# Full-height products for the rest channels, and equal weights side by side

## The chip, the cores and the metric

The kernel runs on one core of a Trainium2 chip. The metric is the device time of one execution in microseconds (us), as the median of several runs. All inputs are drawn at random with a fixed seed.

## What is computed

A tensor x of 2 x 4096 tokens with 192 channels goes through three steps. The first is a causal convolution over 7 tokens, with one softmaxed row of taps for each of 8 groups of 24 channels. The second and third are two gated layers of the same shape, 192 to 2048 to 192, with different gates.

```python
def _moe_ref(x, w_in, w_out):
    h = x @ w_in                          # 8192 x 192 by 192 x 2048
    relu6 = np.clip(h + 3.0, 0.0, 6.0)
    g = h * relu6 / 6.0
    return (g @ w_out).astype(np.float32)

def _moe2_ref(x, w_in, w_out):
    h = x @ w_in
    g = np.where(h > 0.0, h, np.exp(np.minimum(h, 0.0)) - 1.0)
    return (g @ w_out).astype(np.float32)
...
    x = attn_out.reshape(B * S, D)
    x = _moe_ref(x=x, **moe_kwargs)
    return _moe2_ref(x=x, **moe2_kwargs)
```

The result is wanted in float32. The weights of the layers arrive as 64-bit floats and are rounded on the chip.

## The kernel before

**Tiles.** Tokens are worked in 16 blocks of 512 (256 of each batch), hidden channels in 16 chunks of 128. One block in one chunk of one layer is a *slot*; there are 512. A slot's first product gives h (128 hidden channels by 512 tokens, `mm1`, line 359, its matmuls on line 368). `gate` (line 371) makes g of it, with one or two ScalarE steps into a tile u and one VectorE step. `split_g` (line 383) makes the parts gh (ScalarE) and gl (VectorE). `mm2` (line 392) multiplies these by the second weights, on lines 401 to 405 in layer 1 (five matmuls of 512 columns) and on lines 413 and 416 in layer 2 (eight matmuls, of 384 and 192 columns in turn).

**Parts.** Each float32 operand is split exactly into a high and a low part of the type float32r, and a product is the sum of high x high, high x low and low x high in float32 PSUM. Of the 192 input channels, the first 128 are the tiles opA (high) and opB (low), against the weights wi-h (high) and wi-l (low). The remaining 64, the *rest channels*, fill only half of the 128 rows. They stand twice over the partitions: opC (`lh`) has the low parts on rows 0 to 63 and the high parts on rows 64 to 127, opD (`hl`) the other way round. Their weights wi-r stand as high over low for the even chunks and as low over high for the odd ones.

So a chunk has five matmuls: wi-h with opA, wi-l with opA, wi-h with opB, and two for the rest. For an even chunk, wi-r with opC at full height gives both mixed products, and the upper-left half of wi-r (rows 0 to 63) with the same rows of opD gives high x high, at half height. For an odd chunk it is wi-r with opD at full height and rows 64 to 127 of wi-r with those of opC.

```python
if f % 2 == 0:
    todo = [(w["h"], A), (w["l"], A), (w["h"], Bt), (w["r"], lh), (w["r"][LO], hl[LO])]
else:
    todo = [(w["r"][UP], lh[UP]), (w["r"], hl), (w["h"], A), (w["l"], A), (w["h"], Bt)]
```

**Order.** `two` (line 591) works two slots at a time, the even chunk and the odd one: both first products, then the second products of the two slots before. As an even chunk ends with its half-height matmul and an odd one begins with its own, the two stand together, one on the upper and one on the lower half of the rows. h has two buffers (`ps_h`, line 91), so a chunk's first matmul waits until the gate of the chunk two slots earlier has read its h. Side work (decoding weights, the convolution, evacuations, splits of layer 1's output) is put beside the slots by `run_jobs` (line 450), which counts VectorE's and ScalarE's columns. Layer 1 is worked up to six blocks ahead; then blocks of layer 2 and layer 1 take turns. In the first 94 slots (`OWN`, line 26, some 230 us) the framework's scheduler may reorder instructions on each engine; after them the order written in the program stands. In these slots all weights are decoded, on VectorE and ScalarE. The taps of the first two blocks are done on TensorE (line 257, tile psc), those of the others on VectorE (tile acc).

Lines recorded as L50 are all VectorE and ScalarE instructions, which pass through the counting class `Meter`; they are told apart by their tiles.

Of the kernel before, what the change touches and what calls it, by code (L numbers as in the profile page):

```python
# [30 lines left out]
HB = NB // 2  # L31
# [1 line left out]


class Meter:
    """An engine whose instructions are counted, in columns."""

    def __init__(self, engine, fixed):
        self.engine, self.fixed, self.work = engine, fixed, 0
# [14 lines left out]

@with_exitstack
def conv_moe_moe2(ctx: ExitStack, tc: tile.TileContext, x, weight, w_in1, w_out1, w_in2, w_out2, out):
    """Causal per-head taps, then two gated layers, block of tokens by block.

    Products: an operand is split exactly into float32r hi + lo (12 bits each)
    and hi*hi + hi*lo + lo*hi accumulate in float32 PSUM. Channels 0..127 are  # L60
    operands A (hi) and B (lo); channels 128..191 ("r") stand twice over the
    partitions, C (hi) and D (lo), against weights stacked as [hi; lo].

    The layers' weights come as float64 bits (two 32-bit words each) and are
    rounded to float32 on chip.
    """
    nc = tc.nc
    B, S, D = x.shape
    H, K = weight.shape
# [31 lines left out]
    three = const.tile([P, 1], F32, name="three")  # L101
    taps = const.tile([P, 2, K], F32, name="taps")

# [1 line left out]
    def word(raw, i):  # L105
        return raw.rearrange("p (n two) -> p n two", two=2)[:, :, i]

    def decode(raw, n, meanwhile):
        """float64 -> float32. The exponent is moved by a product with 2^-112 on
        the high word (its top 8 exponent bits are a float32 exponent), the three  # L110
        low exponent bits and the mantissa by a shift; the low word gives the
        three last mantissa bits, rounded."""
        xw = tmp.tile([P, NB], F32, name="xw", tag="xw")
        act.mul(xw[:, :n], word(raw, 1).bitcast(F32), 2.0 ** -112)
        c = tmp.tile([P, NB], I32, name="cw", tag="cw")
        vec.tensor_scalar(out=c[:, :n], in0=word(raw, 0).bitcast(U32), scalar1=2.0 ** -29, scalar2=7.0,
                          op0=ALU.mult, op1=ALU.min)
        yield
        yield from meanwhile
        xi = xw.bitcast(I32)  # L120
        vec.scalar_tensor_tensor(out=c[:, :n], in0=xi[:, :n], scalar=3, in1=c[:, :n],
                                 op0=ALU.logical_shift_left, op1=ALU.bitwise_or)
        yield
        vec.scalar_tensor_tensor(out=xi[:, :n], in0=xi[:, :n], scalar=SIGN, in1=c[:, :n],
                                 op0=ALU.bitwise_and, op1=ALU.bitwise_or)
        yield
        return xw
# [18 lines left out]
        return t[:, :n]  # L146

    def split_w(item, f):
        """Chunks a..e-1 of the hidden channels. The r rows of w_in come with the even
        chunks on the lower partitions and the odd ones on the upper; in wi the even  # L150
        chunks stand as [hi; lo], the odd ones as [lo; hi]."""
        kind, l, a, e = item
        if kind == "out":
            v = f[:, :(e - a) * D].rearrange("p (f e) -> p f e", f=e - a)
            w = wo[l][:, a:e]
            act.copy(w[:, :, 0:D], v)
            yield
            for c0, c1, to in (((0, P, 2 * P), (P, D, D)) if l == 0 else ((0, D, D),)):
                vec.tensor_tensor(out=w[:, :, to:to + c1 - c0], in0=v[:, :, c0:c1],
                                  in1=w[:, :, c0:c1].bitcast(F32), op=ALU.subtract)  # L160
            yield
            return
        w = {k: v[:, a * P:e * P] for k, v in wi[l].items()}
        if kind == "in":
            f = f[:, :(e - a) * P]
            act.copy(w["h"], f)
            yield
            vec.tensor_tensor(out=w["l"], in0=f, in1=w["h"].bitcast(F32), op=ALU.subtract)
        else:
            f = f[:, :(e - a) // 2 * P].rearrange("p (f c) -> p f c", c=P)  # L170
            r = w["r"].rearrange("p (f two c) -> p two f c", two=2, c=P)
            for k, h in enumerate((LO, UP)):
                act.copy(r[h, k], f[h])
            yield
            for k, h, o in ((0, LO, UP), (1, UP, LO)):
                vec.tensor_tensor(out=r[o, k], in0=f[h], in1=r[h, k].bitcast(F32), op=ALU.subtract)
        yield

# [1 line left out]
    def load_taps():  # L180
        raw = const.tile([H, K], F32, name="traw")
        nc.scalar.dma_start(raw, weight)
# [22 lines left out]
        vec.tensor_copy(taps, pt)  # L205
        yield

# [1 line left out]
    # The r channels of batch 0 stand on the lower half of the partitions, those of batch 1 on the upper.  # L209
    x_sb = {}  # L210
    xT = {}
    opnd = {}
# [36 lines left out]
        return a.rearrange("p n t -> p (n t)")  # L249

    def taps_tensor(b, part):
        """The taps as diagonal matrices, in full float32."""
        q = xT[b, part]
        ps = ps_o.tile([P, NB], F32, name="psc", tag="po")
        for n in range(SEG[part]):
            for k in range(K):
                nc.tensor.matmul(ps[:, n * HB:(n + 1) * HB], diag[k], q[:, n, k:k + HB],  # L257
                                 start=k == 0, stop=k == K - 1)
            yield
        return ps  # L260
# [30 lines left out]
    CONV = 2 * K + 6  # L291

    def ring():
        """Operands of one block in one layer: A hi and B lo of channels 0..127;
        the r channels as [lo; hi] and [hi; lo] over the partitions."""
        A = op.tile([P, NB], F32R, name="opA", tag="opA")
        Bt = op.tile([P, NB], F32R, name="opB", tag="opB")
        lh = op.tile([P, NB], F32R, name="opC", tag="opC")
        hl = op.tile([P, NB], F32R, name="opD", tag="opD")
        return A, Bt, lh, hl  # L300
# [4 lines left out]
        yield from transposes(b, pool, tag)  # L305

    def ring():
        """Operands of one block in one layer."""
        A = op.tile([P, NB], F32R, name="opA", tag="opA")
        Bt = op.tile([P, NB], F32R, name="opB", tag="opB")  # L310
        C = op.tile([P, NB], F32R, name="opC", tag="opC")
        Dt = op.tile([P, NB], F32R, name="opD", tag="opD")
        return A, Bt, C, Dt

# [1 line left out]
    SIXTH = 1.0 / 6.0  # L316

    ys = {}

    def evac1(b, p0, p1):  # L320
        """Layer 1's sum, over six (its gate was not divided). p1 holds the r
        channels' hi and lo weight parts on its two halves."""
        y0 = yp.tile([P, NB], F32, name="y0", tag="y0")
        act.mul(y0, p0, SIXTH)
        yield
# [29 lines left out]
            nc.sync.dma_start(out[t0:t0 + P, :], o)  # L355
            yield

# [1 line left out]
    def mm1(l, b, f):  # L359
        A, Bt, lh, hl = opnd[l, b]  # L360
        w = {k: v[:, f * P:(f + 1) * P] for k, v in wi[l].items()}
        h = ps_h.tile([P, NB], F32, name="h", tag="h")
        if f % 2 == 0:
            todo = [(w["h"], A), (w["l"], A), (w["h"], Bt), (w["r"], lh), (w["r"][LO], hl[LO])]
        else:
            todo = [(w["r"][UP], lh[UP]), (w["r"], hl), (w["h"], A), (w["l"], A), (w["h"], Bt)]
        for i, (k, m) in enumerate(todo):
            nc.tensor.matmul(h, k, m, start=i == 0, stop=i == len(todo) - 1)  # L368
        return h
# [49 lines left out]
                for step in (lo, hi) if last else (hi, lo):  # L419
                    step(j)  # L420

# [1 line left out]
    slots = [(0, 0, f) for f in range(STAG)]  # L423
    for f in range(STAG, NF + STAG, 2):
        slots += [(0, 0, f), (0, 0, f + 1)] * (f < NF) + [(0, 1, f - STAG), (0, 1, f - STAG + 1)]
# [16 lines left out]
                    yield  # L442

    def job(gen, n, a, e):
        """A generator of n steps, run after slot a and before slot e."""
        jobs.append([e if callable(e) else lambda: e, a, gen, n, 0])

    debt = [0, 0]

    def run_jobs(s, before):  # L450
        """Side work next to slot s: what is due; in the steady part, each job's even share;
        in the first part as much as keeps the engines at the tensor engine's pace."""
        for i, (eng, w) in enumerate(zip((vec, act), before)):
            debt[i] = min(max(debt[i] - PACE, -PACE), -PACE // 2) + eng.work - w

# [26 lines left out]
        return at[l, 0, a] + (LAG if kind == "out" else 0)  # L482

    def when(i):
        """The slot before which item i is to be there; layer 2's come evenly, ahead of their need."""
        if i >= len(items):
            return 0
        if i < N1:
            return due(items[i]) - LEAD
        return min(due(items[i]) - LEAD, W2[0] + (W2[1] - W2[0]) * (i - N1) // (len(items) - N1))  # L490
# [26 lines left out]
    ready = [0]  # L517

    def prepare():
        """The weights in the order of need, each item's split beside the next one's decoding."""  # L520
        last = iter(())
        for i, item in enumerate(items):
            ahead(i)
# [65 lines left out]
            gs[s] = split_g(raw_g.pop(s))  # L589

    def two(s):
        """Two chunks' first products, so that their half-height ones stand together,
        then the second products of the two before."""
        w = vec.work, act.work
        both = range(s, min(s + 2, NS))
        hs = [mm1(*slots[i]) for i in both]
# [59 lines left out]
```

## Time and profile before

| | before |
|---|---|
| runs | 1274.56, 1274.86, 1274.91 us |
| median | 1274.86 us |
| span of the profiled execution | 1273.5 us |
| TensorE busy (PE) | 1262.9 us, 99%, 6044 matmuls |
| weight loads (PEld) | 973.0 us, 76%, 6044 loads |
| VectorE busy (DVE) | 907.5 us, 71% |
| ScalarE busy (ACT) | 922.1 us, 72% |
| granted TensorE clock | 1.00 over the span |

The span runs from the first instruction to the last; the profiled execution gives no other time of its own. PE stands for TensorE's matmuls and PEld for its weight loads, which are instructions of their own; DVE is VectorE and ACT is ScalarE. A matmul's record begins when it starts; its end is modelled, and records of successive matmuls overlap. The distance from one start to the next therefore says what a matmul takes of TensorE's time, and its record's duration does not.

### The profile page before, as it was taken

To read this page: it belongs to the slowest core of one execution; us is meant where nothing else is said; L and a number is where in the kernel's file an instruction comes from. 1 tells how busy PE (TensorE), PEld (TensorE's weight loads), DVE (VectorE), ACT (ScalarE), POOL (GpSimd) and SP (SyncE) were. 2 spreads that over 40 slices of the span, in tenths; PEclk is the share of its full clock that TensorE was granted. 3 is DMA by queue.
4 is the path that set the end of the run, shared out by engine and by line. 5 is a ranking of instruction groups with operands and counts; after the bars stand their busy time and mean duration, and the time that the engine had idled before them with its cause. 6 is when DMAs were issued, how large, how long until landed. Compare 5 with 4: busy or idle time off the path is not lost.

```text
span 1273.5 us, 17036 instructions
## 1 busy us (share of the span) xinstructions
PE 1262.9 (99%) x6044; PEld 973.0 (76%) x6044; DVE 907.5 (71%) x1557; ACT 922.1 (72%) x1651; POOL 9.5 (1%) x44
## 2 busy tenths in 40 slices
PE   8999999999999999999999999999999999999998
PEld 6777777777787777878778787777877778888887
DVE  7999999766667676676766767667676656666665
ACT  5768777686775867758677585776867677787786
POOL 0000000000000000000000000000000000000000
PEclk9999999999999999999999999999999999999999
DMA  5322110000000000000000000000000000000000
GB/s 166 94 77 59 54 38 13 1 1 26 1 2 24 1 25 2 10 16 1 25 1 23 3 1 26 1 26 1 1 13 1 13 1 8 7 13 13 14 13 13
DMA packets 34581, 26.26 MB, mean 21 GB/s; under 512 B 10816, under 2 KB 33344, under 8 KB 34496
## 3 DMA queue, kind: packets, MB, share of 16 engines
q1 hardware_dynamic: 34480, 25.18, 6.9%
q8 instruction: 47, 0.77, 0.2%
q14 instruction: 38, 0.31, 0.1%
q10 hardware_dynamic: 16, 0.00, 0.0%
HBM read 18.87 MB, written 6.29 MB: 20 GB/s over the span
## 4 chain that ended last, share of the span: by engine, by line
PE 98%; DVE 1%; ACT 0%; DMA 0%; issue 0%; SPq 0%; DVEq 0%
PE h L368 50%; PE po L413 15%; PE po L416 7%; PE p L405 5%; PE p L403 5%; PE p L401 5%; PE p L402 5%; PE p L404 5%; PE psx L229 1%; PE psc L257 0%; DMA x_sb<-in_x_dram 0%; DVE acc L50 0%; ACT u L50 0%; DVE cw L50 0%; DVE diag L50 0%
## 5 line engine op out<-in xcount | busy, mean ns | idle before, releaser
L50 DVE SCALAR_TENSOR_TENSOR g<-u,h 128x512 f32<-128x512 f32 x512 | 351.0, 686 | 322.0 <-ACT u L50 319.9
L50 DVE TENSOR_TENSOR gl<-g,gh 128x512 fp32r<-128x512 f32 x512 | 350.6, 686 | 30.7 <-ACT gh L50 22.3
L50 ACT CAST gh<-g 128x512 fp32r<-128x512 f32 x512 | 314.3, 614 | 45.6 <-DVE g L50 44.0
L50 ACT ACTIVATE u<-h,three 128x512 f32<-128x512 f32 x256 | 175.7, 688 | 183.4 <-PE h L368 182.7
L413 PE MATMUL po<-wo,gh 128*128 128x384 f32 x1024 | 302.2, 358 | 0.0
L416 PE MATMUL po<-wo,gl 128*128 128x192 f32 x1024 | 255.7, 252 | 0.2 <-DVE gl L50 0.2
L50 ACT ACTIVATE u<-h 128x512 f32<-128x512 f32 x256 | 151.3, 591 | 78.7 <-PE h L368 76.1
L416 PEld LDWEIGHTS po<-wo,gl 128*128 128x128 f32 x1024 | 194.9, 191 | 5.4 <-DVE gl L50 0.5
L413 PEld LDWEIGHTS po<-wo,gh 128*128 128x128 f32 x1024 | 192.4, 188 | 5.5
L50 ACT ACTIVATE u<-u 128x512 f32<-128x512 f32 x256 | 161.9, 632 | 8.2
L368 PE MATMUL h<-opD,wi1r 64*128 64x512 f32 (+1 forms) x256 | 119.3, 496 | 0.0
L368 PE MATMUL h<-opD,wi0r 128*128 128x512 f32 (+1 forms) x256 | 118.3, 495 | 0.0
L50 DVE SCALAR_TENSOR_TENSOR acc<-xT,taps,acc 128x256 f32<-128x256 f32 (+1 forms) x180 | 107.0, 602 | 0.0
L368 PEld LDWEIGHTS h<-opD,wi0r 128*128 128x128 f32 (+1 forms) x256 | 47.4, 185 | 76.9 <-issue 76.9
L368 PEld LDWEIGHTS h<-opD,wi1r 64*128 64x128 f32 (+1 forms) x256 | 47.3, 185 | 76.9 <-issue 76.9
L368 PE MATMUL h<-opC,wi1r 128*128 128x512 f32 (+1 forms) x256 | 105.3, 441 | 0.0
L368 PE MATMUL h<-opC,wi0r 64*128 64x512 f32 (+1 forms) x256 | 104.9, 443 | 0.0
L368 PE MATMUL h<-opA,wi1h 128*128 128x512 f32 x256 | 104.0, 406 | 0.0
L368 PE MATMUL h<-opA,wi0h 128*128 128x512 f32 x256 | 102.1, 399 | 0.0
L405 PE MATMUL p<-gl,wo 128*128 128x512 f32 x256 | 102.0, 398 | 0.0
L368 PE MATMUL h<-opA,wi1l 128*128 128x512 f32 x256 | 101.7, 397 | 0.0
L368 PE MATMUL h<-opA,wi0l 128*128 128x512 f32 x256 | 101.7, 397 | 0.0
(86 smaller groups left out, 1648.6 us busy)
## 6 DMA issues: line engine op xcount, KB each, us to landing
raw<-in_moe_w_out_dram SPq DMA_DIRECT2D x16, 384.0 KB, 3.2
out_dram<-o SPq DMA_DIRECT2D x64, 96.0 KB, 1.7
x_sb<-in_x_dram SPq DMA_DIRECT2D x32, 128.0 KB, 2.6
raw<-in_moe_w_in_dram SPq DMA_DIRECT2D x7, 512.0 KB, 3.8
xr_sb<-in_x_dram SPq DMA_DIRECT2D x32, 64.0 KB, 2.3
raw<-in_moe_w_in_dram SPq DMA_DIRECT2D x8, 256.0 KB, 3.9
raw<-in_moe_w_in_dram SPq DMA_DIRECT2D x4, 128.0 KB, 3.2
traw<-in_weight_dram ACTq DMA_DIRECT2D x1, 0.2 KB
```

Source lines behind the costliest of these rows:

```text
L50: return fn(*args, **kw)
L229: nc.tensor.transpose(ps[:, j * P:(j + 1) * P], src, ident)
L368: nc.tensor.matmul(h, k, m, start=i == 0, stop=i == len(todo) - 1)
L401: nc.tensor.matmul(p0, w0h, gh, start=first, stop=False)
L402: nc.tensor.matmul(p0, w0l, gh, start=False, stop=False)
L403: nc.tensor.matmul(p1, wr, gh, start=first, stop=False)
L404: nc.tensor.matmul(p0, w0h, gl, start=False, stop=last)
L405: nc.tensor.matmul(p1, wr, gl, start=False, stop=last)
L413: nc.tensor.matmul(a[j][:, 0:2 * D], gh[:, j * P:(j + 1) * P], w, start=first, stop=last)
L416: nc.tensor.matmul(a[j][:, 0:D], gl[:, j * P:(j + 1) * P], w[:, 0:D], start=False, stop=False)
```

## The change

The list of a chunk's matmuls becomes the same for even and odd chunks. The half-height matmul of the rest channels becomes a full-height one: wi-r with opC and wi-r with opD, both over 128 rows. The full-height product with opD also adds low x low, a part that was left out before. The two matmuls with wi-h now follow each other, and so do the two with wi-r. The diff also takes out comments and docstrings, by which the lines between 57 and `mm1` are numbered one higher; lines 368 to 590 keep their numbers.

```diff
     def mm1(l, b, f):
...
         A, Bt, lh, hl = opnd[l, b]
         w = {k: v[:, f * P:(f + 1) * P] for k, v in wi[l].items()}
         h = ps_h.tile([P, NB], F32, name="h", tag="h")
-        if f % 2 == 0:
-            todo = [(w["h"], A), (w["l"], A), (w["h"], Bt), (w["r"], lh), (w["r"][LO], hl[LO])]
-        else:
-            todo = [(w["r"][UP], lh[UP]), (w["r"], hl), (w["h"], A), (w["l"], A), (w["h"], Bt)]
+        todo = [(w["h"], A), (w["h"], Bt), (w["l"], A), (w["r"], lh), (w["r"], hl)]
         for i, (k, m) in enumerate(todo):
             nc.tensor.matmul(h, k, m, start=i == 0, stop=i == len(todo) - 1)
         return h
```

What this does to the order of instructions shows at three places. The first is TensorE in the steady part, the first products of one pair of chunks of layer 1 (h_2542 is the even chunk's h, h_2548 the odd one's). Before:

```order
L368 MATMUL h_2542<-opA_2132,wi0h_88 128x512
L368 MATMUL h_2542<-opA_2132,wi0l_89 128x512
L368 MATMUL h_2542<-opB_2133,wi0h_88 128x512
L368 MATMUL h_2542<-opC_2134,wi0r_90 128x512
L368 MATMUL h_2542<-opD_2135,wi0r_90 128x512
L368 MATMUL h_2548<-opC_2134,wi0r_90 128x512
L368 MATMUL h_2548<-opD_2135,wi0r_90 128x512
L368 MATMUL h_2548<-opA_2132,wi0h_88 128x512
L368 MATMUL h_2548<-opA_2132,wi0l_89 128x512
L368 MATMUL h_2548<-opB_2133,wi0h_88 128x512
```

The last matmul of h_2542 and the first of h_2548 are the half-height ones (the size shown is that of the output). Now:

```order
L368 MATMUL h_2542<-opA_2132,wi0h_88 128x512
L368 MATMUL h_2542<-opB_2133,wi0h_88 128x512
L368 MATMUL h_2542<-opA_2132,wi0l_89 128x512
L368 MATMUL h_2542<-opC_2134,wi0r_90 128x512
L368 MATMUL h_2542<-opD_2135,wi0r_90 128x512
L368 MATMUL h_2548<-opA_2132,wi0h_88 128x512
L368 MATMUL h_2548<-opB_2133,wi0h_88 128x512
L368 MATMUL h_2548<-opA_2132,wi0l_89 128x512
L368 MATMUL h_2548<-opC_2134,wi0r_90 128x512
```

One matmul of the odd chunk, opD with wi0r, follows behind these rows. Both chunks now have the same order, and the odd one's rest products stand at its end.

The second place is TensorE at the first pair of chunks of all, around the convolution's taps on TensorE (psc). Before:

```order
L257 MATMUL psc_310<-xT0_279,diag0_103 128x256 x3
L368 MATMUL h_290<-opA_99,wi0h_88 128x512
L368 MATMUL h_290<-opA_99,wi0l_89 128x512
L368 MATMUL h_296<-opC_101,wi0r_90 128x512
L368 MATMUL h_296<-opD_102,wi0r_90 128x512
L368 MATMUL h_296<-opA_99,wi0h_88 128x512
L368 MATMUL h_296<-opA_99,wi0l_89 128x512
L257 MATMUL psc_310<-xT0_279,diag0_103 128x256
L368 MATMUL h_290<-opB_100,wi0h_88 128x512
L368 MATMUL h_290<-opC_101,wi0r_90 128x512
L368 MATMUL h_290<-opD_102,wi0r_90 128x512
L368 MATMUL h_296<-opB_100,wi0h_88 128x512
```

Now:

```order
L368 MATMUL h_290<-opA_99,wi0h_88 128x512
L368 MATMUL h_296<-opA_99,wi0h_88 128x512
L258 MATMUL psc_310<-xT0_279,diag0_103 128x256
L258 MATMUL psc_310<-xT0_279,diag1_104 128x256 x2
L368 MATMUL h_290<-opB_100,wi0h_88 128x512
L368 MATMUL h_290<-opA_99,wi0l_89 128x512
L368 MATMUL h_290<-opC_101,wi0r_90 128x512
L368 MATMUL h_290<-opD_102,wi0r_90 128x512
L368 MATMUL h_296<-opB_100,wi0h_88 128x512
L368 MATMUL h_296<-opA_99,wi0l_89 128x512
L368 MATMUL h_296<-opC_101,wi0r_90 128x512
L368 MATMUL h_296<-opD_102,wi0r_90 128x512
```

The products with opA and with the rest channels that stood ahead of the first one with opB now stand behind it.

The third place is VectorE just after, at the gates g of this pair. Before:

```order
L50 SCALAR_TENSOR_TENSOR g_302<-u_303,h_290 128x512
L50 TENSOR_SCALAR acc1_318<-xT1_285,taps_98 128x256
L50 SCALAR_TENSOR_TENSOR g_332<-u_333,h_296 128x512
L50 SCALAR_TENSOR_TENSOR acc1_318<-xT1_285,taps_98,acc1_318 128x256
L50 TENSOR_TENSOR gl_338<-g_302,gh_336 128x512
```

Now:

```order
L50 SCALAR_TENSOR_TENSOR g_302<-u_303,h_290 128x512
L50 TENSOR_SCALAR acc1_318<-xT1_285,taps_98 128x256
L50 TENSOR_TENSOR wi0l_89<-xw_259,wi0h_88 128x512
L50 SCALAR_TENSOR_TENSOR acc1_318<-xT1_285,taps_98,acc1_318 128x256
L50 SCALAR_TENSOR_TENSOR g_332<-u_333,h_296 128x512
L50 SCALAR_TENSOR_TENSOR acc1_318<-xT1_285,taps_98,acc1_318 128x256
L50 TENSOR_TENSOR gl_338<-g_302,gh_336 128x512
```

The low part of one piece of weights (wi0l) is taken ahead of the second gate. A few more steps of VectorE and ScalarE change places within the first 40 us; from there on both engines, and GpSimd and the DMA queue throughout, have the same instructions in the same order as before.

## Rows read from the trace of the kernel before

**Rows 1.** The page: the span, then engine, busy us (share), instructions
```profile
span 1273.5 us, 17036 instructions
PE 1262.9 (99%) x6044; PEld 973.0 (76%) x6044; DVE 907.5 (71%) x1557; ACT 922.1 (72%) x1651; POOL 9.5 (1%) x44
```

**Rows 2.** The page: the chain that ended last, shares by engine and by line
```profile
PE 98%; DVE 1%; ACT 0%; DMA 0%; issue 0%; SPq 0%; DVEq 0%
PE h L368 50%; PE po L413 15%; PE po L416 7%; PE p L405 5%; PE p L403 5%; PE p L401 5%; PE p L402 5%; PE p L404 5%; PE psx L229 1%; PE psc L257 0%; DMA x_sb<-in_x_dram 0%; DVE acc L50 0%; ACT u L50 0%; DVE cw L50 0%; DVE diag L50 0%
```

**Rows 3.** Groups by form: line, engine, tiles, rows*columns, form, count, busy us, mean ns
```profile
L368 PE MATMUL h<-opA,wi0l 128*128 128x512 f32 x256 | 101.7, 397 | 0.0
L368 PE MATMUL h<-opD,wi0r 64*128 64x512 f32 x128 | 63.0, 492 | 0.0
```

**Rows 4.** Timeline of TensorE, a pair of layer 1: start us, duration us, instruction
```profile
619.10 0.39 PE L368 MATMUL h<-opA,wi0h 128*128 128x512 f32 x1
619.10 0.19 PEld L368 LDWEIGHTS h<-opA,wi0l 128*128 128x128 f32 x1
...
619.79 0.39 PE L368 MATMUL h<-opC,wi0r 128*128 128x512 f32 x1
620.12 0.18 PEld L368 LDWEIGHTS h<-opD,wi0r 64*128 64x128 f32 x1 [0.36 <-issue]
620.12 0.49 PE L368 MATMUL h<-opD,wi0r 64*128 64x512 f32 x1
...
620.12 0.49 PE L368 MATMUL h<-opC,wi0r 64*128 64x512 f32 x1
...
620.54 0.50 PE L368 MATMUL h<-opD,wi0r 128*128 128x512 f32 x1
...
620.88 0.40 PE L368 MATMUL h<-opA,wi0h 128*128 128x512 f32 x1
...
621.58 0.39 PE L401 MATMUL p<-gh,wo 128*128 128x512 f32 x1
...
623.93 0.39 PE L368 MATMUL h<-opA,wi0h 128*128 128x512 f32 x1
```

**Rows 5.** Timeline of TensorE in the start, around a lone half-height matmul
```profile
32.18 0.40 PE L368 MATMUL h<-opB,wi0h 128*128 128x512 f32 x1
...
32.51 0.49 PE L368 MATMUL h<-opC,wi0r 64*128 64x512 f32 x1
...
32.93 0.50 PE L401 MATMUL p<-gh,wo 128*128 128x512 f32 x1
...
33.27 0.40 PE L402 MATMUL p<-gh,wo 128*128 128x512 f32 x1
...
33.50 0.40 PE L368 MATMUL h<-opD,wi0r 128*128 128x512 f32 x1
...
33.74 0.39 PE L368 MATMUL h<-opC,wi0r 128*128 128x512 f32 x1
```

**Rows 6.** Windows: us, each engine's busy us (instructions), granted clock, DMA share, GB/s
```profile
20.00:220.00 200.00, 200.00 (x838) 145.18 (x837) 187.35 (x348) 149.02 (x270) 2.86 (x8) 1.00 0.22 63
...
180.00:200.00 20.00, 20.00 (x88) 14.61 (x87) 19.72 (x37) 16.43 (x30) 0.44 (x2) 1.00 0.22 62
```

**Rows 7.** VectorE's waits, 20 to 220 us: us in total, times, longest
```profile
DVE g L50 <- ACT u L50: 8.7, 25, 0.9
```

**Rows 8.** Timeline at the start of a layer-2 block: ScalarE, VectorE, TensorE
```profile
576.64 0.60 ACT L50 ACTIVATE u<-h 128x512 f32<-128x512 f32 x1 [0.48 <-PE h L368]
...
580.44 0.69 DVE L50 SCALAR_TENSOR_TENSOR g<-u,h 128x512 f32<-128x512 f32 x1 [1.82 <-ACT u L50]
...
580.89 0.49 PE L368 MATMUL h<-opD,wi1r 64*128 64x512 f32 x1
...
581.18 0.49 PE L368 MATMUL h<-opC,wi1r 64*128 64x512 f32 x1
```

**Rows 9.** Timeline of VectorE: the low part of block 0's first operand
```profile
19.98 0.67 DVE L50 TENSOR_TENSOR opB<-psc,opA 128x512 fp32r<-128x512 f32 x1
```

## The prediction

> **What bounds the kernel now.** I read the page's table of busy times first: TensorE is busy for 1262.9 of 1273.5 us, VectorE and ScalarE for 71% and 72% [rows 1]. The chain that ended last says the same: 98% of it is TensorE, and half of the whole chain is line 368, the first products, which the change rewrites [rows 2]. So what one TensorE slot costs is paid nearly in full at the end, and the question is how long the slots around the half-height matmuls are. A record's own duration does not tell that, because matmuls overlap: the half-height ones have a mean of 492 ns [rows 3], yet a full-height one starts every 0.23 us. I therefore read distances between starts in the timeline.
>
> One pair of chunks stands in [rows 4]. The ten second products run from 621.58 to 623.93, where the next pair begins: 2.35 us, 0.235 each. The ten first products, with as many columns each, run from 619.10 to 621.58: 2.48 us. The difference sits in one place: from opC full height (619.79) over the two halves (both 620.12) and opD full height (620.54) to the next opA (620.88) pass 1.09 us, for four matmuls. The two halves do run together, starting within 0.01 us. But before them stand 0.33 us, after them 0.42, and one matmul further still 0.34. The rows of the weight loads show why: a load normally starts together with the matmul ahead of its own (the load for wi0l at 619.10, the start of the matmul on wi0h; it is used 0.23 us later), while the first half's load starts at 620.12, together with its own matmul, after 0.36 us without a load ("issue": nothing else was waited for). Around a change of height the load is no longer hidden behind a matmul.
>
> **The change, part by part.**
>
> *Two halves become two full-height matmuls.* There are four groups of 128 half-height matmuls, one of which is shown [rows 3]: 512, in 256 pairs. Now: 1.09 us for the four matmuls around each pair. After: four full-height starts at the plain distance, 4 x 0.235 = 0.94. That is 0.15 less per pair, and 256 x 0.15 = **38.4 us less**. The opposite price, two slots where the halves shared one, is in this sum: the 0.94 counts all four. A row of a full-height rest product right behind another one is rare in the trace, but there is one, in the start: opD full at 33.50, opC full at 33.74, 0.24 apart [rows 5]. Starts are shown to 0.01 us, so the 0.15 may be off by 0.01: 2.6 us each way.
>
> By the Trainium skill ("TensorE: Matmul & The Clock Gate", Part 3: Packing small matmuls) matmuls in different row groups run side by side and a pack lasts one matmul plus some 4 ns for each further one. Of this the trace bears out the start, within 0.01 us, but not the length: by that rule alone the halves would cost one slot, giving them up would add an estimated 0.23 us per pair, and the kernel would end some 59 us later.
>
> *The order inside a chunk.* wi-h against opA, then opB, then wi-l, then the rest. No matmul is added, and no load falls away in the program: each matmul call brings its own load, before and after, 6044 of each [rows 1]. Plain starts are 0.23 to 0.24 apart whichever weights follow, so I put this at nothing; the second load of the same weights hides behind the matmul ahead as any other does. What it would be if not is a rival below.
>
> *VectorE and ScalarE.* Their work is the same, so a faster TensorE leaves them less time. It matters between 20 and 220 us, where the weights are decoded: VectorE is busy 187.35 of 200 us, and 19.72 of 20 between 180 and 200 [rows 6]. About 41 pairs pass there (200 / 4.83, the sum of the two halves of a pair above), so TensorE wants to be done 41 x 0.15 = 6.2 us sooner; VectorE has 12.65 us without work, of which 8.7 is waiting for ScalarE's u, which follows TensorE and shrinks with it [rows 7]. Bounds: 0, if the idle time gives way, and 6.2, if VectorE keeps its present pace. Only in the shown 20 us does its work (19.72) exceed what TensorE would leave (20 - 4.1 x 0.15 = 19.4), by 0.3. I take **+0.5**, near the lower end. After 240 us the gates come well ahead but for the one place that follows.
>
> *A wait that is there already.* Near the start of a layer-2 block the odd chunk's first matmul waits for the gate of the odd chunk before it, because there are two h buffers: the upper half starts at 581.18 instead of beside the other at 580.89, right behind the g that ran from 580.44 for 0.69 [rows 8]. This stands twelve times in the timeline, 0.29 us each, 3.5 in all. The chain on ScalarE that leads to this g (the u steps, and the evacuations yr between them) begins with the h of the even chunk, at 576.64. That chunk's last matmul now starts 4 x 0.235 = 0.94 into its pair instead of 1.02 (620.12 - 619.10) and lasts 0.40 instead of 0.49 [rows 4], so h is there 0.17 us sooner. TensorE wants the odd chunk's first matmul when it does now: a pair is 0.15 shorter, but the odd chunk stands 5 x 0.235 = 1.17 into it, 0.15 later. So each wait shrinks by 0.17: 12 x 0.17 = **2.0 less**. Bounds: -3.5 if it vanishes, +1.8 if it grows by a pair's 0.15 each time.
>
> *The start.* opB is now the second operand that TensorE asks for. Block 0's opB is written from 19.98 for 0.67 us [rows 9], while TensorE already multiplies by block 0's opA; the old order had wi-l and rest products to put there. So up to 0.67 us of waiting, in a stretch where the half-height matmuls of the old order stood singly and lost time too. One split of weights also moves ahead of a gate on VectorE; that gate is needed only behind the tap products that TensorE has next, which cover it. I take **+0.3**, bounds 0 and 0.67. The tail (last matmuls, evacuation, store) is untouched.
>
> **Sum.** -38.4 + 0.5 - 2.0 + 0.3 = -39.6. The profiled execution spans 1273.5 [rows 1], and the median of the runs is 1274.9, so 1.4 us lie outside the span and stay. 1273.5 - 39.6 + 1.4 = 1235.3, so **1235 us**, 3.1% faster. With the lower bounds (-41.0, 0, -3.5, 0) it is 1230; with the upper ones (-38.4, +6.2, +1.8, +0.7) 1245. The upper one leaves the main term where it is, since the 0.15 comes out the same in every pair that I read.
>
> **Rivals.**
>
> *VectorE takes over in the start.* For it: 94% busy over 200 us, 99% in one stretch. Against it: the list of waits has none of TensorE's in that stage, and part of its idle time is owed to TensorE. It would take back the 6.2 us: 1235.3 - 0.5 + 6.2 = 1241. It decides if its idle time in that stage stays above about 7 us.
>
> *Slower: the extra time belongs to the rest products, not to the change of height.* The four matmuls take 1.09 where three slots (the halves sharing one) would be 0.705: 0.385 extra. If all of it hung on the operands C and D or on wi-r, then two full-height matmuls instead of two joint halves would cost one more slot: +0.235 x 256 = 60 us, 1335. It decides against the change once 39% of the extra stays (0.15 of 0.385). This is also where the Trainium skill's rule on packs, named above, leads. For it: in the steady part these gaps stand only beside rest products. Against it: in the start a lone half is followed by second products, which know nothing of C, D or wi-r, and the 0.42 and 0.34 are there all the same (32.51, 32.93, 33.27), while the two full-height rest products behind them are 0.24 apart [rows 5].
>
> *Much faster: equal weights in a row save the exchange.* Two places per chunk, 1024 in all. At the granted clock of 1.00 [rows 6], the 2.4 GHz level, 512 columns at one a cycle would be 0.213 us; the start distance is 0.235, so at most 0.021 can go at each: 21.5 us, 1214. Against it: the loads stay in the program, nothing in the trace shows a load left out, and no two neighbours have equal weights now, so the case is not seen.
>
> **Chances.** The forecast 0.90; VectorE taking over 0.06; equal weights saving time 0.02; slower 0.02. The range 1230 to 1245 takes in the forecast's bounds and the first rival. Faster by over 0.2% (2.5 us, about what a measurement of this kernel can tell): 0.97; within 0.2%: 0.01; slower: 0.02.
>
> **What the new profile would show.** No half-height form; all of line 368's matmuls near 395 ns, with starts 0.23 apart through all ten, so about 2.34 us from a pair's start to its second products; the 0.36 us without a load gone; VectorE's busy share up only because the span is shorter, over 96% between 20 and 215. Wrong would be starts of 0.3 or more around opC and opD (the slower rival), starts under 0.225 at opB or opD (the faster one), or TensorE's list of waits naming VectorE's g before 220 us.

## The result, and the profile after

The changed kernel takes 1234.39 us (median of 4 runs, 1234.29 to 1234.47) beside 1274.8 us for the kernel before (four runs, 1274.56 to 1274.91). The ratio is 0.9683, with a 95% interval of 0.9669 to 0.9697: 3.2% faster, against a forecast of 1235 within 1230 to 1245. The profiled execution spans 1232.6 us, 40.9 less than before [rows 1].

The page of the changed kernel, its span and its table of busy times (engine, us, share, instructions):

```profile
span 1232.6 us, 17033 instructions
PE 1223.2 (99%) x6044; PEld 1038.7 (84%) x6044; DVE 905.6 (73%) x1557; ACT 923.7 (75%) x1651; POOL 10.9 (1%) x44
```

TensorE is still busy for 99% of the span, with as many matmuls and loads as before. The loads' busy time has grown from 973.0 to 1038.7 us in a shorter span, since loads that overlapped each other before now stand apart: in each of 253 pairs the two halves' loads overlapped by 0.18 us and the two behind them by 0.08, 66 us in all.

The timeline of TensorE in one pair of layer 1 (start us, duration us, instruction), which answers to [rows 4]:

```profile
599.00 0.39 PE L368 MATMUL h<-opA,wi0h 128*128 128x512 f32 x1
...
599.71 0.39 PE L368 MATMUL h<-opC,wi0r 128*128 128x512 f32 x1
599.94 0.39 PE L368 MATMUL h<-opD,wi0r 128*128 128x512 f32 x1
600.17 0.40 PE L368 MATMUL h<-opA,wi0h 128*128 128x512 f32 x1
...
600.88 0.40 PE L368 MATMUL h<-opC,wi0r 128*128 128x512 f32 x1
601.11 0.40 PE L368 MATMUL h<-opD,wi0r 128*128 128x512 f32 x1
601.35 0.39 PE L401 MATMUL p<-gh,wo 128*128 128x512 f32 x1
...
603.69 0.40 PE L368 MATMUL h<-opA,wi0h 128*128 128x512 f32 x1
```

The ten first products run from 599.00 to 601.35, 2.35 us instead of 2.48, and the ten second products to 603.69, 2.34. From opC to the next chunk's opA the even chunk needs 0.46 us for two matmuls (599.71, 599.94, 600.17); before, the even chunk's two and the odd chunk's two took 1.09 together. No gap is left beside the rest products.

The gain can be read off along the program, at the first product of pair 8 and of pair 48 (pairs counted from 0). The kernel before:

```profile
62.55 0.39 PE L368 MATMUL h<-opA,wi0h 128*128 128x512 f32 x1
...
258.60 0.39 PE L368 MATMUL h<-opA,wi1h 128*128 128x512 f32 x1
```

The changed kernel:

```profile
59.89 0.39 PE L368 MATMUL h<-opA,wi0h 128*128 128x512 f32 x1
...
249.94 0.40 PE L368 MATMUL h<-opA,wi1h 128*128 128x512 f32 x1
```

Up to pair 8 it is 2.66 us ahead; over the 40 pairs up to pair 48 it gains another 6.00, which is 0.150 for each; from there to the end of the span 32.3 more, over 208 pairs, 0.155 for each.

### The profile page after: what moved, and what is told of

Its sections match the earlier page's. It is cut to its first block, busy times and chain, and to the rows that moved or that the text cites. A ratio compares the mean times of both kernels' runs of the same rounds, so it can differ in the third digit from the quotient of the medians.

```text
span 1232.6 us, 17033 instructions
## 1 busy us (share of the span) xinstructions
PE 1223.2 (99%) x6044; PEld 1038.7 (84%) x6044; DVE 905.6 (73%) x1557; ACT 923.7 (75%) x1651; POOL 10.9 (1%) x44
## 4 chain that ended last, share of the span: by engine, by line
PE 97%; ACT 2%; DVE 1%; issue 0%; DMA 0%; SPq 0%; DVEq 0%; ACTq 0%
PE h L368 48%; PE po L413 16%; PE po L416 7%; PE p L405 5%; PE p L404 5%; PE p L403 5%; PE p L401 5%; PE p L402 5%; PE psx L230 1%; ACT u L50 1%; PE psc L258 1%; ACT opC L50 0%; DMA x_sb<-in_x_dram 0%; ACT opD L50 0%; DVE g L50 0%
## 5 line engine op out<-in xcount | busy, mean ns | idle before, releaser
L413 PEld LDWEIGHTS po<-wo,gh 128*128 128x128 f32 x1024 | 192.3, 188 | 5.3
L368 PE MATMUL h<-opC,wi0r 128*128 128x512 f32 x256 | 101.6, 397 | 0.2 <-ACT opC L50 0.2
L368 PE MATMUL h<-opB,wi1h 128*128 128x512 f32 x256 | 101.6, 397 | 0.0
L401 PE MATMUL p<-gh,wo 128*128 128x512 f32 x256 | 101.6, 397 | 0.0
L405 PE MATMUL p<-gl,wo 128*128 128x512 f32 x256 | 101.5, 397 | 0.0
L368 PE MATMUL h<-opB,wi0h 128*128 128x512 f32 x256 | 101.5, 396 | 0.0
L403 PE MATMUL p<-gh,wo 128*128 128x512 f32 x256 | 101.5, 396 | 0.0
L402 PE MATMUL p<-gh,wo 128*128 128x512 f32 x256 | 101.5, 396 | 0.0
L404 PE MATMUL p<-gl,wo 128*128 128x512 f32 x256 | 101.5, 396 | 0.0
```

The costliest lines, as they stand in the source:

```text
L401: nc.tensor.matmul(p0, w0h, gh, start=first, stop=False)
L402: nc.tensor.matmul(p0, w0l, gh, start=False, stop=False)
L403: nc.tensor.matmul(p1, wr, gh, start=first, stop=False)
L404: nc.tensor.matmul(p0, w0h, gl, start=False, stop=last)
L405: nc.tensor.matmul(p1, wr, gl, start=False, stop=last)
L413: nc.tensor.matmul(a[j][:, 0:2 * D], gh[:, j * P:(j + 1) * P], w, start=first, stop=last)
```

## The experiments

Theory H: a matmul over half the rows among full ones costs a fixed time at the change of height, where loads are not hidden; the change takes this away. Rival O: part of the gain comes from equal weights side by side. Rival R: the lost time belonged to the rest products. Rival P: only halves that run together pay. The starts of the changed kernel above already speak against R.

**Height alone.** full_old_order keeps the order of the kernel before at full height:

```diff
-        todo = [(w["h"], A), (w["h"], Bt), (w["l"], A), (w["r"], lh), (w["r"], hl)]
+        todo = [(w["h"], A), (w["l"], A), (w["h"], Bt)]
+        rest = [(w["r"], lh), (w["r"], hl)]
+        todo = todo + rest if f % 2 == 0 else rest + todo
```

> Full height as in the changed kernel, but each chunk's matmuls in the order of the kernel before (wi-h, wi-l, wi-h; the odd chunk's rest products first). Theory H (the gain is the change of row height that falls away): all of the 40.4 us stays, 1234.4, give or take 1.5 for what the scheduler makes of the start. Rival O (part of the gain comes from equal weights side by side): clearly above, 1240 or more; if nearly all came from there, up to 1275.

Measured: 1234.17 us (4 runs, 1234.08 to 1234.23), ratio to the kernel before 0.9679, interval 0.9662 to 0.9695. The whole gain is there without the new order.

**Order alone.** half_new_order keeps the halves and moves only the matmul with opB:

```diff
-            todo = [(w["h"], A), (w["l"], A), (w["h"], Bt), (w["r"], lh), (w["r"][LO], hl[LO])]
+            todo = [(w["h"], A), (w["h"], Bt), (w["l"], A), (w["r"], lh), (w["r"][LO], hl[LO])]
...
-            todo = [(w["r"][UP], lh[UP]), (w["r"], hl), (w["h"], A), (w["l"], A), (w["h"], Bt)]
+            todo = [(w["r"][UP], lh[UP]), (w["r"], hl), (w["h"], A), (w["h"], Bt), (w["l"], A)]
```

> The halves stay and still stand together, but wi-h with opA and wi-h with opB now follow each other. Theory H: 1274.8, give or take 1.5, with 1.09 us for the four matmuls around each pair of halves. Rival O: faster than that, by 0.02 us for each of 512 places of equal weights, so 1264.

Measured: 1275.06 us (10 runs, 1274.73 to 1275.15), ratio 0.9999, interval 0.9990 to 1.0009. The order is worth nothing that can be measured, and 1264 is excluded.

**No equal neighbours.** no_equal is the changed kernel with its five matmuls in another order:

```diff
-        todo = [(w["h"], A), (w["h"], Bt), (w["l"], A), (w["r"], lh), (w["r"], hl)]
+        todo = [(w["h"], A), (w["r"], lh), (w["h"], Bt), (w["r"], hl), (w["l"], A)]
```

> The changed kernel's ten matmuls per pair of chunks, in an order in which no two neighbours have the same weights (wi-h opA, wi-r opC, wi-h opB, wi-r opD, wi-l opA). Theory H: 1234.4, give or take 1.5, starts 0.234 us apart. Rival O: slower by what equal weights are worth; if 0.01 us at each of 1024 places, 1245.

Measured: 1234.81 us (4 runs, 1234.48 to 1234.97), ratio 0.9683, interval 0.9669 to 0.9698. Its timeline of TensorE, one chunk and the next one's first:

```profile
600.66 0.40 PE L368 MATMUL h<-opA,wi0h 128*128 128x512 f32 x1
600.89 0.40 PE L368 MATMUL h<-opC,wi0r 128*128 128x512 f32 x1
601.13 0.39 PE L368 MATMUL h<-opB,wi0h 128*128 128x512 f32 x1
601.36 0.40 PE L368 MATMUL h<-opD,wi0r 128*128 128x512 f32 x1
601.60 0.40 PE L368 MATMUL h<-opA,wi0l 128*128 128x512 f32 x1
601.83 0.39 PE L401 MATMUL p<-gh,wo 128*128 128x512 f32 x1
```

Starts are 0.23 to 0.24 apart here, where the weights change each time, and in the changed kernel, where they stay the same at two places of a chunk. Rival O falls.

**96 rows.** rows_96 takes 96 rows for the even chunk's last matmul (its low x low part is left out for a part of the channels):

```diff
+        if f % 2 == 0:
+            todo[-1] = (w["r"][0:96], hl[0:96])
```

> As the changed kernel, but the even chunk's last matmul takes 96 of the 128 rows (it leaves out half of the low x low part, which the kernel before left out whole). If the price hangs on the halves of the array being used apart, 96 rows from row 0 on cost a plain slot: 1234.4. If any change in the number of rows costs what a lone half does in the start (0.33 + 0.42 + 0.34 instead of three times 0.234, 0.38 more), 256 of them add 97 us: 1332.

Measured: 1234.60 us (4 runs, 1234.34 to 1235.06), ratio 0.9682, interval 0.9668 to 0.9697. The timeline of TensorE:

```profile
604.60 0.40 PE L370 MATMUL h<-opC,wi0r 128*128 128x512 f32 x1
604.84 0.40 PE L370 MATMUL h<-opD,wi0r 96*128 96x512 f32 x1
605.08 0.39 PE L370 MATMUL h<-opA,wi0h 128*128 128x512 f32 x1
```

Fewer rows as such cost nothing: a matmul over 96 rows among those over 128 starts 0.24 after the one ahead of it, and the next one 0.24 later. So 96 rows take a plain slot, and 64 do not; other sizes were not tried.

**A lone half.** lone_half_even puts the even chunk's half-height matmul back into the changed kernel, without a partner:

```diff
+        if f % 2 == 0:
+            todo[-1] = (w["r"][LO], hl[LO])
```

> As the changed kernel, but the even chunk's last matmul is the half-height one of the kernel before, with no other half beside it. Theory H: a lone half has the same starts around it as a pair of halves, 0.32, 0.42 and 0.34 instead of three times 0.234, 0.38 more; 256 of them: 1234.4 + 97 = 1332. Rival R (the extra time belongs to the rest products, of which there is one full-height one less): 1234 or less. Rival P (only halves that run together pay): 1234.

Measured: 1328.00 us (2 runs), ratio 1.0416, interval 1.0395 to 1.0437: 93.6 us above the changed kernel, 0.366 for each half. The timeline of TensorE and its loads:

```profile
618.67 0.39 PE L370 MATMUL h<-opC,wi1r 128*128 128x512 f32 x1
618.99 0.18 PEld L370 LDWEIGHTS h<-opD,wi1r 64*128 64x128 f32 x1 [0.36 <-issue]
618.99 0.49 PE L370 MATMUL h<-opD,wi1r 64*128 64x512 f32 x1
...
619.41 0.19 PEld L370 LDWEIGHTS h<-opA,wi1h 128*128 128x128 f32 x1 [0.24 <-DVE gl L50]
619.41 0.50 PE L370 MATMUL h<-opA,wi1h 128*128 128x512 f32 x1
...
619.75 0.40 PE L370 MATMUL h<-opB,wi1h 128*128 128x512 f32 x1
```

These are the same three distances as around a pair of halves: 0.32, 0.42 and 0.34. The load of the half starts with its own matmul at 618.99, and so does the load of the full-height one behind it, at 619.41, although that one is a wi-h matmul and no rest product. There is less full-height rest work than in the changed kernel, and the time is longer by 7.6%. Rivals R and P fall.

**Two lone halves.** lone_half_both does so in both chunks:

```diff
+        if f % 2 == 0:
+            todo[-1] = (w["r"][LO], hl[LO])
+        else:
+            todo[3:] = [(w["r"], hl), (w["r"][UP], lh[UP])]
```

> Both chunks end with their half-height matmul, so no two halves stand together and there are 512 lone ones. The products are those of the kernel before. Theory H: twice the 97 us, 1234.4 + 195 = 1429. Rivals R and P: about 1234, or 1275 if the price goes by the number of half-height matmuls, as in the kernel before.

Measured: 1426.67 us (2 runs), ratio 1.1190, interval 1.1167 to 1.1212: 192.3 us above the changed kernel, 0.376 for each of 512 halves. It computes the products of the kernel before in the same number of matmuls and is 151.7 us slower than it: standing together, as in the kernel before, saves the second visit to half height. The price goes by visits: the change from full height to half height and back, with whatever halves stand between.

**What stands behind TensorE.** skip_low leaves out the product of wi-l with opA:

```diff
-        todo = [(w["h"], A), (w["h"], Bt), (w["l"], A), (w["r"], lh), (w["r"], hl)]
+        todo = [(w["h"], A), (w["h"], Bt), (w["r"], lh), (w["r"], hl)]
```

> Leaves out the product of wi-l with opA, one plain slot in each of 512 chunks, to see what stands behind TensorE. If TensorE stays the bound throughout: 512 x 0.234 = 120 us less, 1114.6. My reading of the start (VectorE busy 188 of 195 us between 20 and 215): there only some 7 of 41 x 0.47 = 19 us can go, so about 12 us come back, 1127, with TensorE waiting for gates before 210 us and hardly after 240.

Measured: 1137.36 us (2 runs), ratio 0.8920, interval 0.8903 to 0.8938: 97.0 us less than the changed kernel, not 120, and 10 above my 1127. A window of the start (us, then PE, PEld, DVE, ACT and POOL busy, granted clock, DMA share, GB/s):

```profile
60.00:100.00 40.00, 38.74 (x156) 27.51 (x155) 38.52 (x74) 30.49 (x55) 0.00 (x0) 1.00 0.20 60
```

TensorE's waits (us in total, times, longest), from 20 to 210 us:

```profile
PE h L368 <- DVE g L50: 2.5, 4, 1.1
PE p L401 <- ACT gh L50: 2.4, 5, 0.7
```

And from 210 to 1130 us:

```profile
PE h L368 <- DVE g L50: 6.7, 13, 1.3
```

The first product of pair 50 in the changed kernel:

```profile
259.24 0.42 PE L368 MATMUL h<-opA,wi1h 128*128 128x512 f32 x1
```

In skip_low:

```profile
250.24 0.41 PE L368 MATMUL h<-opA,wi1h 128*128 128x512 f32 x1
```

In the start VectorE is busy 38.5 of 40 us while TensorE no longer is all the time, and TensorE now waits for VectorE's g and for ScalarE's gh. Pair 50 is 9.0 us earlier, where 50 pairs less two plain slots each would make 23.4: 14.4 us have come back by then, somewhat more than the 12 I expected. The two waits of the list make up 4.9 of these; records overlap (0.39 us long, with starts 0.23 apart), so shorter waits are not in the list, and which engine the other 9.5 are due to was not worked out. Some 8 us come back later, mostly in the waits at the starts of layer-2 blocks, which I had expected to stay small: the wait for the gate of the odd chunk grows from some 0.12 to some 0.6 us in each. So my sum was missing this second place, and most of TensorE's listed waiting for g lies there, not in the start.

**The wait at the block's start.** split_yr cuts the evacuation into yr, whose two ScalarE steps stand in front of the gate's, into two pieces of side work:

```diff
         act.mul(yr[LO], p1[UP], SIXTH)
+        yield
         act.mul(yr[UP], p1[LO], SIXTH)
...
-                    job(evac(ql, qb), 4 - (ql == 0), s + 1, s + 4)
+                    job(evac(ql, qb), 4, s + 1, s + 4)
```

> As the changed kernel, but the two halves of the evacuation into yr are two steps of the side work, which can be put beside different slots, instead of one. The waits near the start of twelve layer-2 blocks (some 0.22 us each beyond plain starts, 2.8 in all) shrink if the two in a row are what holds the gate up: 1232 to 1234. If something else holds it: 1234.4, or later by as much where the second half now delays another gate.

Measured: 1232.01 us (4 runs, 1231.81 to 1232.09), ratio 0.9663, interval 0.9647 to 0.9679: 2.4 us less than the changed kernel and the fastest of all. The intervals of the two ratios overlap; that the 2.4 us are real shows in the traces. At the first product of pair 48 split_yr is only 0.1 us ahead (249.94 above, 249.85 here), and at the end of the span (1230.1 us) 2.5:

```profile
249.85 0.39 PE L369 MATMUL h<-opA,wi1h 128*128 128x512 f32 x1
```

The timeline of the changed kernel at the start of a layer-2 block, ScalarE, VectorE and TensorE with one of its loads, which answers to [rows 8]:

```profile
559.11 1.20 ACT L50 ACTIVATE yr<-p 64x512 f32<-64x512 f32 x2
...
561.63 0.69 DVE L50 SCALAR_TENSOR_TENSOR g<-u,h 128x512 f32<-128x512 f32 x1 [1.82 <-ACT u L50]
...
562.02 0.40 PE L368 MATMUL h<-opD,wi1r 128*128 128x512 f32 x1
...
562.37 0.50 PE L368 MATMUL h<-opA,wi1h 128*128 128x512 f32 x1
...
562.48 0.19 PEld L368 LDWEIGHTS h<-opB,wi1h 128*128 128x128 f32 x1
...
562.71 0.39 PE L368 MATMUL h<-opB,wi1h 128*128 128x512 f32 x1
```

The same place in split_yr:

```profile
558.47 0.59 ACT L50 ACTIVATE yr<-p 64x512 f32<-64x512 f32 x1
...
560.38 0.69 DVE L50 SCALAR_TENSOR_TENSOR g<-u,h 128x512 f32<-128x512 f32 x1 [1.22 <-ACT u L50]
...
561.03 0.39 PE L369 MATMUL h<-opD,wi1r 128*128 128x512 f32 x1
...
561.26 0.40 PE L369 MATMUL h<-opA,wi1h 128*128 128x512 f32 x1
...
561.49 0.40 PE L369 MATMUL h<-opB,wi1h 128*128 128x512 f32 x1
```

With two yr steps (1.20 us) ahead, the gate g ends at 562.32 and opA's matmul starts at 562.37, 0.35 after the matmul ahead of it; the next one follows after 0.34. With one yr step, g ends at 561.07, before opA's matmul could start anyway, and the starts are 0.23 apart. Of the twelve such waits of the changed kernel one is left in split_yr. So the two steps in a row did hold the gate up.

## Why the prediction was right, and where its steps were off

**The main term held.** 0.15 us for each of 256 pairs was the forecast; the stretch from pair 8 to pair 48 gives 0.150, and the starts in nanoseconds give 0.148 (0.321, 0.003, 0.422 and 0.338, less 4 x 0.234, as medians over the 253 pairs whose halves stood together). It is the change of height alone (full_old_order), not the order (half_new_order, no_equal). That the halves shared a slot, and yet cost more than two slots, is shown by the lone halves: a visit to half height costs some 0.37 to 0.38 us beyond its slots, and the slot that a pair shares is worth 0.234, so a pair loses 0.15 against two full-height matmuls. By the Trainium skill ("TensorEngine Tiling (Array Packing)", Key Properties) a change of tiling mode drains TensorE; the loads without cover at 620.12 [rows 4] and at 618.99 and 619.41 in lone_half_even agree. Here the change to half height and back cost 0.37 to 0.38 us. That the price is there at the change of height is shown by the experiments; that the late loads are the whole of it, as the prediction reads them, was not tested by itself.

**VectorE did not take over.** I allowed 0.5 us. From pair 8 to pair 48, the stretch in which VectorE is busiest, nothing was lost. The windows of the changed kernel, which answer to [rows 6], and VectorE's wait for u, which answers to [rows 7]:

```profile
20.00:215.00 195.00, 194.79 (x845) 156.56 (x845) 188.19 (x352) 151.57 (x273) 4.20 (x8) 1.00 0.23 64
175.00:195.00 20.00, 20.00 (x91) 16.14 (x90) 19.95 (x38) 16.39 (x29) 0.82 (x2) 1.00 0.21 59
```

```profile
DVE g L50 <- ACT u L50: 2.9, 7, 0.8
```

VectorE is now busy 188.19 of 195 us, 96.5%, and in one stretch all but 0.05 of 20. Its wait for u has shrunk from 8.7 to 2.9 us: the idle time gave way, as the lower bound had it. TensorE's list of waits from 20 to 220 us names no g of VectorE; its one entry is a wait of 0.2 us for opC. But little is left: 6.8 us without work, hardly under the 7 above which I had given the case to the rival, and skip_low shows that much of a next gain on TensorE is lost there.

**The wait at the block's start was mis-sized.** I forecast that each of the twelve waits would shrink by 0.17, 2.0 us in all. The wait itself did: 562.37 is 0.35 after 562.02, 0.12 more than a plain start, where it was 0.29. What I left out is the matmul behind it: its load starts late too (562.48, not with the matmul ahead), so it starts 0.34 later instead of 0.23, another 0.1. In the kernel before that loss lay in the gaps around the halves. So eleven of the twelve places gained some 0.08 each. At the second place the wait grew to 0.33, which with the matmul behind it makes 0.43 instead of 0.29; the reason stays open:

```profile
265.04 0.40 PE L368 MATMUL h<-opD,wi1r 128*128 128x512 f32 x1
265.60 0.50 PE L368 MATMUL h<-opA,wi1h 128*128 128x512 f32 x1 [0.16 <-DVE g L50]
```

All twelve together gave some 0.7 us instead of 2.0. The stretch behind pair 48 gained 32.3 us; 208 pairs at 0.148 are 30.8, which leaves 1.5: the 0.7 of the waits, and 0.8 in some 4 ns per pair that the four distances do not hold.

**The start was mis-sized, with the wrong sign.** I put it at +0.3; it came out at about -1.5, the 2.66 up to pair 8 less the 1.2 that 8 pairs are worth. 0.3 of this lies ahead of the first product (18.84 before, 18.52 now), in which the two kernels are the same; over all ten traces it starts between 18.42 and 18.84, so this is chance. The rest is in the old order with its halves, as these rows of the timeline of the kernel before show:

```profile
19.58 0.49 PE L368 MATMUL h<-opC,wi0r 64*128 64x512 f32 x1
...
21.79 0.50 PE L368 MATMUL h<-opD,wi0r 64*128 64x512 f32 x1
...
34.06 0.49 PE L368 MATMUL h<-opD,wi0r 64*128 64x512 f32 x1
...
57.52 0.49 PE L368 MATMUL h<-opD,wi0r 64*128 64x512 f32 x1
...
58.42 0.50 PE L368 MATMUL h<-opC,wi0r 64*128 64x512 f32 x1
```

With the one at 32.51 [rows 5] these are six halves that the scheduler had torn apart. Each cost a visit of its own, 0.38, where I had counted half of a pair's 0.148: 6 x 0.38 less 3 x 0.148 makes an estimated 1.8 us. A wait in the new order takes some 0.5 of it back, 0.37 at the matmul itself and 0.1 at the one behind it: in the changed kernel the first matmul with block 1's opC starts 0.60 after the one ahead of it.

```profile
32.39 0.39 PE L403 MATMUL p<-gh,wo 128*128 128x512 f32 x1
32.99 0.50 PE L368 MATMUL h<-opC,wi0r 128*128 128x512 f32 x1 [0.21 <-ACT opC L50]
```

That the halves and not the order cost this time shows in the runs that part the two: pair 8 starts at 59.67 in full_old_order and at 62.45 in half_new_order. I had named these lone halves and not priced them. The wait for opB that I feared hardly came: TensorE ran six tap products in front of it, and the matmul with opB started at 20.40.

**Sum.** -37.9 (256 pairs at 0.148), -1.5 (start), 0 (VectorE), -0.7 (waits) and -0.8 (the few ns per pair) make -40.9, which is the difference of the spans. The forecast, -39.6, was 1.3 short. That it came so close in the total is in part luck: the start came out 1.8 below its term and the waits 1.3 above theirs, and these errors partly cancel. The main term, 38.4 in the forecast, needed no luck.

## What to carry to other kernels

Count a product over half the rows by the distances between starts, through to the second matmul behind it, and not by its work: among full-height matmuls of 512 columns a visit to half height cost 0.37 to 0.38 us here, more than a whole slot (0.234), so it paid to fill the rows with an extra product. Halves that stand together share the visit; if a scheduler tears them apart, each pays alone. Two that share it still lost 0.15 against two full-height products; more than one pair in a visit was not run. When such a change makes the leading engine faster, look at once at what feeds it: here VectorE has 3.5% left in the start, and a ScalarE chain in front of a gate was worth another 2.4 us.

## What I had not expected of the hardware

A matmul that waits for a semaphore costs more than its wait: the one behind it started 0.34 us later instead of 0.234 (562.37 and 562.71 in the changed kernel), and its load began at 562.48, 0.11 behind the waiting matmul's start, where a load otherwise begins with the matmul ahead of its own. And 96 of 128 rows cost a plain slot (0.24), while 64 cost a visit: between these two sizes the price does not grow evenly with the empty rows.
